# Reordering the load queue of a fused scan and feed-forward kernel: an input block ahead of the first turns

## The chip, the cores and the metric

The kernel runs on one core of a Trainium2 chip. The metric is the device time of one execution in microseconds (us). "Fast" runs are those in which the core was not in its slow state. A core has TensorE (PE, matmuls), VectorE (DVE), ScalarE (ACT), GpSimd (POOL) and SyncE (SP), which here issues nearly all transfers. A transfer that transposes on its way (kind DMA_TRANSPOSE) is called a *turn* below.

## The reference, cut to what matters

```python
xn = layernorm(x)                               # x: 2048 x 512, bf16
Bu = xn @ B_bar.T                               # complex: two real products (B_re, B_im)
h[t] = Lam_bar * h[t-1] + Bu[t]                 # scan over the 2048 rows
y = 2 * Re(h @ C.T) + xn * Dskip
out = x + y + (gelu(xn @ w_gate) * (xn @ w_up)) @ w_down
```

The kernel works in four blocks of 512 rows. Block 0 is special: while the weights still arrive, a *first stage* multiplies centred rows, turned on TensorE itself, with the first 896 columns of the gate and up weights. For the other columns, for Bu and for all later blocks, TensorE reads normalized rows that a turn has brought into the layout it needs.

## The kernel before

The program is written as a list of operations. A planner inside the kernel orders VectorE, ScalarE and GpSimd; **TensorE and SyncE keep the order in which the operations are written**. So the source order of the loads is the order of the load queue.

```python
def tr_par():                                   # the parameter turn: 16 x 128 -> 128 x 16
    S.dma(lambda e: e.dma_start_transpose(PAR..., PROW16.ap), ..., tag="tr_par", issue=900.0)
def TR(b, js=range(4)):                         # the turns of block b, one for each 128 rows
    for j in js:
        S.dma(lambda e, ...: e.dma_start_transpose(XNT[b].ap[:, :, 128*j:128*(j+1)], XN[tt % 8].ap), ...)
...
load_W()                                        # the last weight pieces
tr_par()
...                                             # the first stage
TR(0, [0, 1])
...
TR(0, [2, 3])
ld_x(1)                                         # x of block 1, 512 KB
params()                                        # angles from the parameters
tables_dve(None)
load_B()                                        # B_re, B_im (turns), the D row, x of block 2
LN(1, [0, 1]); LN(1, [2, 3])
TR(1)
SKIP(0)
GU(0, [7, 8, 9, 10])                            # gate/up of block 0, waits for all of TR(0)
...
BU(0)                                           # Bu of block 0
```

Of the kernel before, what the change touches and what calls it, by code (L numbers as in the profile page):

```python
# [352 lines left out]
def d_dve_tt2x(n): return 100.0 + 0.52 * n  # L353
# [4 lines left out]
def d_act(n, ptr=0): return 190.0 + 0.833 * n + 90.0 * ptr  # L358
# [3 lines left out]
def build(nc, ins, out):  # L362
    with ExitStack() as es:
# [113 lines left out]
        def ld_x(b):  # L477
            return S.dma(lambda e, b=b: e.dma_start(
                X_all.ap[:, 4 * b:4 * b + 4, :], x2[512 * b:512 * (b + 1), :].rearrange("(j p) d -> p j d", p=128)),
                512 * 1024, writes=X[4 * b:4 * b + 4], tag="ld_x%d" % b)  # L480
# [28 lines left out]
        def tr_par():  # L509
            S.dma(lambda e: e.dma_start_transpose(PAR.ap.rearrange("p q t -> p (q t)").unsqueeze(1), PROW16.ap), 4096,  # L510
                  reads=PROWq, writes=[PAR], tag="tr_par", issue=900.0)
# [7 lines left out]
        def load_T(bufs, nms):  # L519
            for b_, nm in zip(bufs, nms):  # L520
                S.dma(lambda e, b_=b_, nm=nm: e.dma_start_transpose(b_.ap, ins[nm]),
                      1.4 * 512 * 1024, writes=[b_], tag="tr_" + nm, issue=3000.0)

        def load_W():
            ld_w(WG, WGc, ins["B_w_gate"], 2)
            ld_w(WU, WUc, ins["B_w_up"], 2)

        def load_B():
            load_T([A.sub(BBT_all, "BBTc%d" % c, c) for c in range(2)], ("A_B_re", "A_B_im"))
            S.dma(lambda e: e.dma_start(DSKB.ap, ins["A_Dskip"].unsqueeze(0).broadcast_to([128, D])),  # L530
                  128 * 1024, writes=[DSKB], tag="ld_dsk")
            ld_x(2)

        def load_C():
            load_T(CRAW, ("A_C_re", "A_C_im"))
# [15 lines left out]
        def params():  # L551
            S.order_behind(POOL(lambda e: e.tensor_tensor(DTB.ap, EXB.ap, LDT.ap, ALU.pow), 1100, [EXB, LDT], [DTB], "exp_dt"), GATE["pow"])
            V(lambda e: e.tensor_tensor(pa(TH), DTB.ap, LIM.ap, ALU.mult), D_TINY, [DTB, LIM], [PA[TH]], "th")
            V(lambda e: e.tensor_tensor(pa(A_), DTB.ap, LRE.ap, ALU.mult), D_TINY, [DTB, LRE], [PA[A_]], "a")
            POOL(lambda e: e.tensor_tensor(pa(RRr), EXB.ap, pa(A_), ALU.pow), 1100, [EXB, PA[A_]], [PA[RRr]], "exp_a")
            V(lambda e: e.tensor_scalar(w16(0, 4), pa(TH), 1.0 / TWO_PI, None, ALU.mult), D_TINY, [PA[TH]], [W16p[0]])
            V(lambda e: e.tensor_scalar(w16(4, 8), pa(TH), 512.0 / TWO_PI, None, ALU.mult), D_TINY, [PA[TH]], [W16p[1]])
            V(lambda e: e.tensor_scalar(w16(8, 16), w16(0, 8), 0.25, None, ALU.add), D_TINY, W16p[0:2], W16p[2:4])
            V(lambda e: e.tensor_copy(KI.ap, W16.ap), D_TINY, W16p, [KI])
            V(lambda e: e.tensor_tensor(FRC.ap, W16.ap, KI.ap, ALU.subtract), D_TINY, W16p + [KI], [FRC])  # L560
# [34 lines left out]
        def tables_dve(behind):  # L595
            for s in range(KP):
                V(lambda e, s=s: e.tensor_scalar(K1s[s].ap, IOTJ.ap, W16.ap[:, s:s + 1], None, ALU.mult),
                  d_dve_ts4x(512) * 1.3, [IOTJ, W16p[0]], [K1s[s]], "k1", [GATE["evTA"]])
                V(lambda e, s=s: e.scalar_tensor_tensor(F1s[s].ap, IOTJ.ap, W16.ap[:, s:s + 1], K1s[s].ap, ALU.mult, ALU.subtract),
                  d_dve_1x(512), [IOTJ, W16p[0], K1s[s]], [F1s[s]], "f1")  # L600
            S.order_behind(V(lambda e: e.tensor_scalar(A1.ap.bitcast(I32), F1.ap.bitcast(I32), 0x7FFFFFFF, None, ALU.bitwise_and), d_dve_ts4x(2048) * 2, F1s, [A1], "a1"), behind)
# [6 lines left out]
        def stats(b, j):  # L608
            tt = 4 * b + j
            return (V(lambda e: e.bn_stats(ST[tt].ap, X[tt].ap), d_dve_1x(512), [X[tt]], [ST[tt]], "bnst"),  # L610
                    V(lambda e: e.bn_aggr(MVt[b][j].ap, ST[tt].ap), D_TINY, [ST[tt]], [MVt[b][j]], "bnag"))

        def root(b, j0, j1):
            mn, sbq, qb, rq = (cols(t, b, j0, j1) for t in (MN, SBQ, QB, RQ))
            mv = Buf("MV%d_%d_%d" % (b, j0, j1), "sb", MVt[b][j0].lo, MVt[b][j1 - 1].hi, MV[b].ap[:, j0:j1])
            op = V(lambda e: e.tensor_scalar(sbq.ap, mv.ap[:, :, 1], EPS_BF16, None, ALU.add), D_TINY, [mv], [sbq], "sbq")
            GATE["pow"] = POOL(lambda e: e.tensor_tensor(qb.ap, sbq.ap, HALF.ap[:, 0:j1 - j0], ALU.pow), 1100, [sbq, HALF], [qb], "pow")
            POOL(lambda e: e.tensor_copy(mn.ap, mv.ap[:, :, 0]), 200, [mv], [mn], "mn")
            return op, mn, qb, rq

        def recip(qb, rq):
            return V(lambda e: e.reciprocal(rq.ap, qb.ap), 150, [qb], [rq], "rq")

        def norms(b, js, mn, rq, j0):
            last = None
            for j in js:
                tt, i = 4 * b + j, j - j0
                xs = XN[tt % 8]
                last = S.order_behind(V(lambda e, tt=tt, i=i, xs=xs: e.tensor_scalar(
                    xs.ap, X[tt].ap, mn.ap[:, i:i + 1], rq.ap[:, i:i + 1], ALU.subtract, ALU.mult),  # L630
                  d_dve_ts4x(512), [X[tt], mn, rq], [xs], "ln_n"), last)
            return last

        def LN(b, js=range(4)):
            for j in js:
                stats(b, j)
            _, mn, qb, rq = root(b, js[0], js[-1] + 1)
            recip(qb, rq)
            norms(b, js, mn, rq, js[0])
# [23 lines left out]
        def SKIP(b):  # L663
            for tt in range(4 * b, 4 * b + 4):
                xs = XN[tt % 8]
                V(lambda e, tt=tt, xs=xs: e.tensor_tensor(XD[tt].ap, xs.ap, DSKB.ap, ALU.mult),
                  d_dve_tt2x(512), [xs, DSKB], [XD[tt]], "skip")
# [64 lines left out]
        def TR(b, js=range(4)):  # L732
            for j in js:
                tt = 4 * b + j
                S.dma(lambda e, b=b, j=j, tt=tt: e.dma_start_transpose(
                    XNT[b].ap[:, :, 128 * j:128 * (j + 1)], XN[tt % 8].ap),
                    1.6 * 128 * 1024, reads=[XN[tt % 8]], writes=[XTk[b][j]], tag="tr_x%d" % b, issue=1280.0)
# [212 lines left out]
                     d_dve_ts4x(512), [X[j], MVt[0][j]], [XN[j]], "sub")  # L950
        load_par()
        load_W()
        tr_par()
        S.order_behind(ACT(lambda e: e.activation(H0[3].ap[:, 0:D], X[1].ap, ACTF.Copy, scale=-1.0 / D, accum_out=NM1.ap), d_act(512) + 190,
                           [X[1]], [H0[3], NM1], "mean1"), GATE["par"])

# [54 lines left out]
        norms(0, [2], mn0, rq0, 0)  # L1011
        norms(0, [3], mn3, rq3, 3)
        TR(0, [2, 3])
        ld_x(1)
        params()
        tables_dve(None)
        load_B()
        LN(1, [0, 1]); LN(1, [2, 3])
        TR(1)
        SKIP(0)  # L1020
        GU(0, [7, 8, 9, 10])
        GATE["before_gelu"] = [tables_act([GATE["last_gelu"]])]
# [29 lines left out]
def bass_parallel_sum__ssm_conv_s5__geglu_ffn__prompt_kernel(  # L1052
    nc: bass.Bass,
    A_x: bass.AP,
    A_Lambda_re: bass.AP,
    A_Lambda_im: bass.AP,
    A_B_re: bass.AP,
    A_B_im: bass.AP,
    A_C_re: bass.AP,
    A_C_im: bass.AP,  # L1060
    A_log_dt: bass.AP,
    A_Dskip: bass.AP,
    B_x: bass.AP,
    B_w_gate: bass.AP,
    B_w_up: bass.AP,
    B_w_down: bass.AP,
    out: bass.AP,
):
    ins = {
        "A_x": A_x, "A_Lambda_re": A_Lambda_re, "A_Lambda_im": A_Lambda_im,  # L1070
        "A_B_re": A_B_re, "A_B_im": A_B_im, "A_C_re": A_C_re, "A_C_im": A_C_im,
        "A_log_dt": A_log_dt, "A_Dskip": A_Dskip,
        "B_w_gate": B_w_gate, "B_w_up": B_w_up, "B_w_down": B_w_down,
    }
    build(nc, ins, out)
# [28 lines left out]
```

## Time and profile before

| what | value |
|---|---|
| time | 177.46 us (median of 3), 177.29 (median of 6 with the later runs) |
| TensorE busy | 172.1 us of 175.7 |
| last turn of block 0 lands | 16.99 us |
| gate/up matmuls of block 0 start | 18.24 us by the record |

The prediction below shows the main lines. The chain of waits of the kernel before, in order of time (columns: start, duration, engine and line, count), begins like this.

```profile
0.77 3.15 PE PS L932 x7
3.92 0.11 PE PS L939
4.03 0.13 PE PS L679
4.16 0.30 PE PS L939 x4
...
4.57 0.38 PE PS L700 x2
...
11.26 6.93 PE PS L711 x40
18.18 0.05 issue
18.24 5.13 PE PS L842 x23
```

L932 is the warm-up (matmuls on constants), L939 fills, L679 turns on TensorE, L700 and L711 are the first stage, L842 the gate/up matmuls. Seven warm-up matmuls of 512 columns take 3.15 us, 450 ns each: half the later pace. TensorE's clock is not yet open (more on this below). Two things that I passed over: the pace changes *between* 4.16 and 4.57 us in this run, and L842 has **23** records where the program has 24. The "issue" of 0.05 us ahead of it is the trace of a lost record. The first gate/up matmul was at 18.02 us (one matmul of 0.22 us earlier), not 18.24.

### The profile page before, as it was taken

How to read it: one execution, taken by the hardware profiler on the slowest of the kernel's cores; microseconds unless marked ns; L12 is line 12 of the kernel's file. 1: busy time of each engine (PE TensorE's matmuls, PEld its weight loads, DVE VectorE, ACT ScalarE, POOL GpSimd, SP SyncE). 2: the span in 40 equal slices, each digit the busy share in tenths (PEclk: the TensorE clock that was granted, in tenths of full speed). 3: DMA queues.
4: the chain of work that ended last, by engine and by line, in shares of the span. 5: the costliest groups of instructions: out<-in, count | busy, mean ns of one | idle time of the engine just before them, and what ended most of it. 6: DMA issues, size and time to landing. Idle time of an engine off the chain costs nothing.

```text
span 175.7 us, 2494 instructions
## 1 busy us (share of the span) xinstructions
PE 172.1 (98%) x868; PEld 84.0 (48%) x883; DVE 159.8 (91%) x279; ACT 95.5 (54%) x185; POOL 10.7 (6%) x24
## 2 busy tenths in 40 slices
PE   8999999999999999999999999999999999999995
PEld 3545564644544444444644444444464444444454
DVE  6987999996999989889899999989999899999941
ACT  5476677899876898383576792000667970000000
POOL 3122030201000000002100000000000000000000
DMA  5899999695998000002015000002001000000311
GB/s 155 241 320 174 215 178 222 126 132 113 191 298 225 0 4 2 0 30 85 8 39 111 1 0 0 4 0 90 30 0 30 4 0 0 0 0 0 120 64 60
DMA packets 32420, 14.36 MB, mean 82 GB/s; under 512 B 23736, under 2 KB 32408, under 8 KB 32408
## 3 DMA queue, kind: packets, MB, share of 16 engines
q1 hardware_dynamic: 32240, 14.07, 35.5%
q8 instruction: 7, 0.11, 0.3%
q10 hardware_dynamic: 168, 0.13, 0.2%
q14 instruction: 5, 0.04, 0.1%
HBM read 6.46 MB, written 2.10 MB: 49 GB/s over the span
## 4 chain that ended last, share of the span: by engine, by line
PE 98%; issue 1%; DVE 0%
PE PS L883 37%; PE PS L842 32%; PE PS L748 16%; PE PS L711 4%; PE PS L700 3%; PE PS L816 3%; PE PS L932 2%; PE PS L679 1%; PE PS L939 0%; DVE arena L901 0%
## 5 line engine op out<-in xcount | busy, mean ns | idle before, releaser
L883 PE MATMUL PS<-arena 128*128 128x512 bf16 (+3 forms) x317 | 65.9, 366 | 0.3
L842 PE MATMUL PS<-arena 128*128 128x512 bf16 x257 | 57.1, 379 | 0.4
L883 PEld LDWEIGHTS PS<-arena 128*128 128x128 bf16 (+1 forms) x323 | 30.8, 98 | 35.2
L842 PEld LDWEIGHTS PS<-arena 128*128 128x128 bf16 x264 | 25.8, 98 | 30.2
L786 DVE TENSOR_TENSOR_SCAN arena<-arena 128x512 bf16<-128x512 f32 x32 | 38.9, 1255 | 0.0
L857 ACT ACTIVATE arena<-PS 128x512 bf16<-128x512 f32 x33 | 19.8, 599 | 25.8 <-DVE arena L901 16.7
L748 PE MATMUL PS<-arena 128*128 128x512 bf16 (+1 forms) x134 | 28.0, 366 | 0.1
L861 ACT ACTIVATE arena<-PS 128x512 bf16<-128x512 f32 x33 | 19.8, 600 | 5.1 <-PE PS L842 5.1
L875 ACT ACTIVATE PS<-arena 128x512 f32<-128x512 bf16 (+2 forms) x17 | 9.6, 581 | 19.7 <-DVE arena L901 19.0
L748 PEld LDWEIGHTS PS<-arena 128*128 128x128 bf16 x136 | 13.3, 98 | 14.1
L757 ACT ACTIVATE arena<-PS 128x512 bf16<-128x512 f32 x32 | 17.7, 592 | 2.1 <-PE PS L748 2.1
L901 DVE TENSOR_TENSOR arena<-PS,arena 128x512 bf16<-128x512 f32 (+2 forms) x17 | 10.9, 653 | 6.4 <-PE PS L883 6.4
L863 DVE TENSOR_TENSOR arena<-arena 128x512 bf16<-128x512 bf16 x33 | 13.1, 416 | 1.7 <-ACT arena L861 1.6
L775 DVE TENSOR_TENSOR arena<-arena 128x4096 bf16<-128x4096 bf16 (+1 forms) x5 | 9.2, 1859 | 0.8 <-ACT arena L606 0.8
L773 DVE TENSOR_TENSOR arena<-arena 128x4096 bf16<-128x4096 bf16 (+1 forms) x5 | 9.2, 1859 | 0.1
L798 DVE TENSOR_TENSOR arena<-arena 128x4096 bf16<-128x4096 bf16 x4 | 9.2, 2288 | 0.1
L799 DVE TENSOR_TENSOR arena<-arena 128x4096 bf16<-128x4096 bf16 x4 | 9.1, 2284 | 0.0
L720 ACT ACTIVATE arena<-PS,arena 128x256 bf16<-128x256 f32 (+1 forms) x16 | 6.6, 448 | 3.9 <-PE PS L700 2.1
L610 DVE BATCH_NORM_STATS2 arena<-arena 128x6 f32<-128x512 bf16 x12 | 7.7, 679 | 0.1
L711 PE MATMUL PS<-arena 128*128 128x512 bf16 (+1 forms) x40 | 7.1, 336 | 0.0
L723 DVE SCALAR_TENSOR_TENSOR arena<-PS,arena 128x256 bf16<-128x256 f32 (+1 forms) x16 | 6.3, 445 | 0.5 <-PE PS L700 0.5
L700 PE MATMUL PS<-arena 128*128 128x512 bf16 (+1 forms) x28 | 6.2, 349 | 0.2
(96 smaller groups left out, 124.6 us busy)
## 6 DMA issues: line engine op xcount, KB each, us to landing
out_dram<-arena SPq DMA_DIRECT2D x15, 128.0 KB, 1.7
arena<-in_A_x_dram SPq DMA_DIRECT2D x3, 512.0 KB, 5.3
arena<-in_B_w_down_dram SPq DMA_DIRECT2D x1, 1280.0 KB, 7.2
arena<-in_B_w_gate_dram SPq DMA_DIRECT2D x4, 128.0 KB, 3.0
arena<-in_B_w_up_dram SPq DMA_DIRECT2D x4, 128.0 KB, 3.1
arena<-in_B_w_gate_dram SPq DMA_DIRECT2D x1, 480.0 KB, 6.5
arena<-in_B_w_up_dram SPq DMA_DIRECT2D x1, 480.0 KB, 7.4
arena<-arena SPq DMA_TRANSPOSE x25, 3.1
```

The costliest lines, as they stand in the source:

```text
L700: PE(lambda e: e.matmul(dst, XCd(j, k), WGU[:, ws[0]:ws[-1] + 1, k, f0:f1], start=first, stop=k == KD - 1, skip_group_check=True), d_pe([w ...
L711: ins_ = e.matmul(dst, XCd(j, k), WGU[:, :, k, f0:f1], start=(k == 0), stop=(k == KD - 1))
L748: ins_ = e.matmul(PS[bank][:, 128 * j0:128 * j1], BBT[c][dk].ap[:, 128 * s:128 * (s + 1)], XNT[b].ap[:, dk, 128 * j0:128 * j1], start=(dk ...
L757: GATE["evBu"] = ACT(lambda e, bank=bank, k3=k3, s=s, c=c: e.activation(SSc[k3][s][c].ap, PS[bank][:, :], ACTF.Copy), d_act(512), [BANK[ba ...
L786: V(lambda e, g=g, rb=rb, init=init: e.tensor_tensor_scan(g.ap, rb, g.ap, init, ALU.mult, ALU.add), d_dve_scan(512), [g, PA[RRr]] + ([CARc ...
L842: ins_ = e.matmul(PS[bank][0:m, c0:c1], W.ap[:, dk, 128 * ft:128 * ft + m], XNT[b].ap[:, dk, c0:c1], start=(dk == 0), stop=(dk == KD - 1))
L857: GATE["last_gelu"] = ACT(lambda e, bg=bg, kk=kk, m=m: e.activation(GG[kk].ap[0:m, :], PS[bg][0:m, :], ACTF.Gelu_apprx_tanh), d_act(512), ...
L861: ACT(lambda e, bu=bu, kk=kk, m=m: e.activation(UPB[kk].ap[0:m, :], PS[bu][0:m, :], ACTF.Copy), d_act(512), [BANK[bu]], [UPB[kk]], "evU")
L863: V(lambda e, kk=kk, m=m, ft=ft, k2=k2: e.tensor_tensor(HTt[k2][ft].ap[0:m, :], GG[kk].ap[0:m, :], UPB[kk].ap[0:m, :], ALU.mult), d_dve_tt ...
L875: ACT(lambda e: e.activation(PS[bank][:, c0:c1], X[tt].ap[:, c0:c1], ACTF.Copy), d_act(c1 - c0), [X[tt]], [BANK[bank]], "seed")
L883: ins_ = e.matmul(PS[bank][:, c0:c1], l_[:, 128 * j:128 * (j + 1)], r_[:, c0:c1], start=False, stop=last and n == len(ops) - 1, skip_group ...
L901: V(lambda e: e.tensor_tensor(OUTB[ko].ap[:, c0:c1], PS[bank][:, c0:c1], XD[tt].ap[:, c0:c1], ALU.add), d_dve_1x(c1 - c0), [BANK[bank], XD ...
```

## The change

Its intent: bring x of block 1 in earlier, so that VectorE can begin its normalization, and let what is not urgent (parameters, D row) wait. No instruction is added or removed.

```diff
         def load_B():
             load_T([A.sub(BBT_all, "BBTc%d" % c, c) for c in range(2)], ("A_B_re", "A_B_im"))
+
+        def load_skip():
             S.dma(lambda e: e.dma_start(DSKB.ap, ins["A_Dskip"]...
-            ld_x(2)
@@
         load_W()
-        tr_par()
+        ld_x(1)
@@
         TR(0, [2, 3])
-        ld_x(1)
+        tr_par()
         params()
         tables_dve(None)
         load_B()
+        ld_x(2)
         LN(1, [0, 1]); LN(1, [2, 3])
         TR(1)
+        load_skip()
         SKIP(0)
```

## The prediction

> **What bounds the kernel now.** I read the page's busy times first, then the chain that ended last, then three engine timelines of the first 45 us, because the change touches only the order of loads there.
>
> ```profile
> PE 172.1 (98%) x868; PEld 84.0 (48%) x883; DVE 159.8 (91%) x279; ACT 95.5 (54%) x185; POOL 10.7 (6%) x24
> PE 98%; issue 1%; DVE 0%
> ```
>
> The chain of waits is TensorE (PE) from the first microsecond to the last. A busy row alone could hide pipelined idleness, so I check the pace: the same chain lists 49 matmuls of 512 columns in 10.74 us (219 ns each) in every gate/up stage, and 12 of them in 2.60 us (217 ns) elsewhere. The pace is the same in all stages, and the "issue" pieces between them are 0.05 us, about what a missing record leaves. From 18 us to 174 us TensorE therefore streams without a gap, in an order that the program fixes. The only loose place is before 11 us: the early matmuls between 4.57 and 11.26 us are 12 of 256 columns, 16 of 512 and 16 short transposes. At 219 and some 110 and 55 ns that is 5.7 us of streaming in 6.7 us. So at most about 1 us is there to gain, and it hangs on the first rows of x and the weight pieces, which the change doesn't touch.
>
> The second view is the timeline of the load queue (SyncE; columns: start, time that the queue was taken, line, kind, target and source, count).
>
> ```profile
> 7.51 0.51 SPq L489 DMA_DIRECT2D arena<-in_B_w_up_dram  x1
> 8.14 2.37 SPq L510 DMA_TRANSPOSE arena<-arena  x1
> 10.56 5.18 SPq L735 DMA_TRANSPOSE arena<-arena  x4
> 15.79 0.58 SPq L478 DMA_DIRECT2D arena<-in_A_x_dram  x1
> 16.41 3.06 SPq L521 DMA_TRANSPOSE arena<-in_A_B_re_dram  x1
> 19.51 3.60 SPq L521 DMA_TRANSPOSE arena<-in_A_B_im_dram  x1
> 23.16 0.58 SPq L530 DMA_DIRECT2D arena<-in_A_Dskip_dram  x1
> 23.78 0.43 SPq L478 DMA_DIRECT2D arena<-in_A_x_dram  x1
> 24.34 5.13 SPq L735 DMA_TRANSPOSE arena<-arena  x4
> ```
>
> In this order: last weight piece; the turn (DMA transpose) of the parameters; four turns of block 0; x of block 1; B twice; the D row; x of block 2; four turns of block 1. The third view is TensorE's timeline, which says when each is needed.
>
> ```profile
> 11.10 7.09 PE L711 MATMUL PS<-arena 128*128 128x512 bf16 x40
> 18.24 5.13 PE L842 MATMUL PS<-arena 128*128 128x512 bf16 x23
> 23.20 1.48 PE L816 MATMUL PS<-arena 128*128 128x192 bf16 x16
> 24.52 14.00 PE L748 MATMUL PS<-arena 128*128 128x512 bf16 x70
> ```
>
> The gate/up matmuls of block 0 (L842, at 18.24) need all four turned tiles of block 0. The Bu matmuls (L748, at 24.52) need B_re at once, B_im after the 16 matmuls of the first component (about 28 us), and block 1's turns after all 32 of block 0 (about 31.5 us).
>
> Asking each issue for its time to landing, I get: last weight piece 14.9 us (7.51 + 7.4), parameter turn 15.2, the turns of block 0 at 15.5, 15.9, 16.4, 17.0, x of block 1 at 19.6, B_re 23.8, B_im 25.4, D row 27.7, x of block 2 at 29.1, turns of block 1 at 30.2, 30.7, 31.1, 31.6. So the slack now is 1.2 us at the gate/up matmuls (18.2 - 17.0), some 0.8 us at B_re, and near none at the last turn of block 1. Landings march on in issue order: this queue is a backlog.
>
> **What the Trainium skill says.** "DMA: Bandwidth & Descriptors", section "Queues, rings and completion order": on each DMA engine the descriptors of one queue are consumed in ring order. The trace agrees: issues at 7.51, 8.14 and 10.56 land at 14.9, 15.2 and 15.5. Hence what stands in front delays what stands behind. The same page, section "Issuing engines are not separate DMA queues": all transfers share 16 engines; the trace shows them booked full from 9 to 16 us (DMA share 0.97 to 1.42 in one-microsecond windows), so there is no second road. "Perfetto Trace Analysis", section on the HWDGE DMA instruction: the profiled piece of a DMA is the making of its descriptors, not the move. The trace agrees: 0.5 us for a weight piece that lands 7.4 us later. "TensorE: Matmul & The Clock Gate", section "Back-to-back issue gap", gives about 131 ns a matmul of 512 columns sustained, and 216 ns isolated; this trace shows 217 to 219 sustained, so I take TensorE as having nothing to give.
>
> **The change part by part.** No instruction is added or removed; four loads change places.
>
> (a) x of block 1 (512 KB) goes from behind block 0's turns to before them. It is issued at about 8.1 us and starts to move when the weights are done, at 14.9. Its cost I take from its twin: x of block 2 landed 1.4 us after the D row in front of it; at the 320 GB/s of 10 to 14 us it is 1.6. So it lands at about 16.4 instead of 19.6, 3.2 us earlier.
>
> (b) The turns of block 0 now stand behind those 1.5 us. The twin again: the four turns of block 1 behind x of block 2 landed 1.1 us after it, then every 0.45 us, 2.5 us for the last. Then block 0's last turn lands at 16.4 + 2.5 = 18.9 us, where TensorE wants it at 18.24. That is a stall of **0.6 us**. If only the 1.5 us are added to the old 17.0, it is 18.5 and 0.3 us. As TensorE never waits afterwards, nothing later absorbs it.
>
> (c) The parameter turn goes behind block 0's turns. They wait for normalized rows (the last is written at 13.0), so they issue from about 9.9 to 15 us; the parameter turn issues to 16 or 17.5 and lands at 18.5 to 19.5 in place of 15.2. What hangs on it is a GpSimd power (1.02 us), a few small VectorE (DVE) instructions and the angle tables. Those ended at 30.2 us, because VectorE was full, not because the parameters were late: th was there at 16.52, but the last multiply of the tables came only at 28.8. VectorE now has block 1's statistics (four of 0.65 us) to do meanwhile, so tables and statistics swap. Estimate 0 on the chain.
>
> (d) B is issued at 16 to 17.5 instead of 16.41, but with x of block 1 already landed. Its two issues took 3.06 and 3.60 us behind that load; C, the same shape on an empty queue, landed 4.4 us after issue. So B_re lands at about 21 to 23.5, still before 24.5. Cost 0.
>
> (e) The D row goes last. Its use (L666) is at 33.7 us and has no near consumer on TensorE. Cost 0. Block 1's turns come earlier, but TensorE was not waiting for them. Gain 0.
>
> (f) The program order on VectorE and ScalarE is made by the kernel's own planner, which assumes that loads move at 350 bytes per ns plus 2 us. By its rule x of block 1 would be there about 13.8 us into the span (3.34 MB of earlier loads in 9.55 us, 1.5 us for itself, 2 us, and the start at 0.74), 2.6 us before my 16.4. If it puts a statistics instruction in front of a product of the first stage, VectorE (in order) stands still until the load is there. Those products free PSUM banks: bank 2 was free at 17.0 for a matmul at 18.24, so 1.2 us can be lost unseen, and more while TensorE is stalled for (b). I count 0.1 us on average.
>
> Sum: 177.46 + 0.6 + 0.1 = about **178.1 us**.
>
> **Rivals.** First, nothing happens: the turns still land by 18.2, as 17.0 + 1.2 would. For it: the last turn needed just 2.5 us from issue, and the issues start 0.6 us earlier. Against it: the DMA engines are full. It gives 177.4. Second, VectorE becomes the new wait, by (f): VectorE sits up to 2.6 us and TensorE loses that less 1.2, plus a knock-on at the first output stage, whose C coefficients are ready at 71.65 us and used at 63.85 + 44 x 0.217 = 73.4, only 1.7 us later. That gives 179 to 180.5. For it: the statistics have the room (VectorE had one hole, 15.3 to 16.5); against it: the planner may fill exactly that hole, and then almost nothing is lost. Third, a gain: the intent is surely an earlier block 1 and a fuller VectorE. VectorE at 91% looks near the limit, but the chain shows it with 0%, so an earlier VectorE buys nothing. At best 177.0.
>
> **Range and chances.** The terms span -0.4 (noise; the runs lay at 177.1 to 177.93) to +2.3. I give 177.1 to 179.7. A change of 2% is 3.55 us: a gain of that size doesn't exist on a full TensorE, and a loss would take rivals one and two at their worst together. Faster 0.01, same 0.94, slower 0.05.
>
> **What would show it.** Block 0's gate/up matmuls start at 18.5 to 19 instead of 18.24, with a wait for a DMA before them; after that TensorE runs gapless and every later stage is shifted by the same amount. x of block 1 lands near 16.4, the parameter turn after 18, B_re before 24.5. The prediction is wrong if TensorE waits at the Bu matmuls (B late), if VectorE shows a hole at 14 to 16.5 in front of a statistics instruction (rival two), or if the first output stage waits for the C coefficients.

## The result, and the profile after

The changed kernel took **177.69 us** (median of 6, 177.45 to 177.9) against 177.29 (median of 6, 177.08 to 177.93). The ratio is 1.0018, with a 95% interval of 0.9999 to 1.0037. A ratio is the mean time of one kernel's fast runs over that of the other's of the same rounds, so it is not quite the ratio of the medians. By the ratio the loss is 0.3 us (0.0018 x 177.3), half of the 0.64 us that I had forecast; the interval just includes no loss at all, so this set alone does not show one.

The load queue after (same view as in the prediction):

```profile
7.51 0.65 SPq L489 DMA_DIRECT2D arena<-in_B_w_up_dram  x1
8.20 1.63 SPq L478 DMA_DIRECT2D arena<-in_A_x_dram  x1
10.03 6.16 SPq L736 DMA_TRANSPOSE arena<-arena  x4
16.32 1.15 SPq L510 DMA_TRANSPOSE arena<-arena  x1
17.51 2.82 SPq L521 DMA_TRANSPOSE arena<-in_A_B_re_dram  x1
```

The issue of x of block 1 took 1.63 us where it took 0.58 before; what it waits for, no view says. It landed 7.9 us after its start, at 16.07; the turns landed at 16.57, 17.03, 17.52 and 17.99. So far as foretold, though the turns follow faster. Now the chain of waits after:

```profile
0.77 3.14 PE PS L933 x7
3.92 0.11 PE PS L940
4.02 0.25 PE PS L680
4.28 0.43 PE PS L940 x4
4.70 0.57 PE PS L701 x2
...
11.94 6.93 PE PS L712 x40
18.86 5.18 PE PS L843 x24
24.04 1.32 PE PS L817 x16
25.36 13.83 PE PS L749 x72
```

Line numbers from here on have moved by one. The gate/up matmuls follow the first stage **without a gap**. In this run they did not wait for the turns at all. What is late is the first stage itself: it begins its second part at 11.94 instead of 11.26, and the delay arises before 7 us, in matmuls that ran at half pace (four fills in 0.43 us, not 0.30; a pair of 256 columns in 0.57, not 0.38). Both kernels have issued exactly the same loads up to 8 us. The profiles of before and after thus differ by 0.68 us for a reason that the change cannot have made, while the foretold stall is missing. A verdict from these two profiles would be wrong either way.

The Trainium skill explains the opening: "TensorE: Matmul & The Clock Gate", section "Part 1: The HAM clock gate", says that the array starts at half clock and opens after a busy window of 3.4 us, and that this window is free-running, so that the moment differs from run to run. The traces agree that the moment differs: by the spacing of the matmuls the half pace ended at about 4.2 us in the profile of before and at about 6.7 in that of after, a wider spread than the half microsecond either way that the page gives.

### The profile page after: what moved, and what is told of

It reads as the page before. It is cut to its first block, busy times and chain, and to the rows that moved or that the text cites. A ratio compares the mean times of both kernels' runs of the same rounds, so it can differ in the third digit from the quotient of the medians.

```text
span 176.3 us, 2506 instructions
## 1 busy us (share of the span) xinstructions
PE 173.7 (99%) x883; PEld 84.6 (48%) x883; DVE 160.4 (91%) x279; ACT 95.4 (54%) x185; POOL 9.7 (6%) x24
## 4 chain that ended last, share of the span: by engine, by line
PE 99%; DVE 0%; issue 0%
PE PS L884 37%; PE PS L843 32%; PE PS L749 16%; PE PS L712 4%; PE PS L701 3%; PE PS L817 3%; PE PS L933 2%; PE PS L680 1%; PE PS L940 0%; DVE arena L902 0%
## 5 line engine op out<-in xcount | busy, mean ns | idle before, releaser
L843 PE MATMUL PS<-arena 128*128 128x512 bf16 x264 | 58.1, 379 | 0.0
L749 PE MATMUL PS<-arena 128*128 128x512 bf16 (+1 forms) x136 | 28.1, 366 | 0.0
L712 PE MATMUL PS<-arena 128*128 128x512 bf16 (+1 forms) x40 | 7.1, 336 | 0.0
L701 PE MATMUL PS<-arena 128*128 128x512 bf16 (+1 forms) x28 | 6.9, 380 | 0.0
```

The costliest lines, as they stand in the source:

```text
L701: PE(lambda e: e.matmul(dst, XCd(j, k), WGU[:, ws[0]:ws[-1] + 1, k, f0:f1], start=first, stop=k == KD - 1, skip_group_check=True), d_pe([w ...
L712: ins_ = e.matmul(dst, XCd(j, k), WGU[:, :, k, f0:f1], start=(k == 0), stop=(k == KD - 1))
L749: ins_ = e.matmul(PS[bank][:, 128 * j0:128 * j1], BBT[c][dk].ap[:, 128 * s:128 * (s + 1)], XNT[b].ap[:, dk, 128 * j0:128 * j1], start=(dk ...
L843: ins_ = e.matmul(PS[bank][0:m, c0:c1], W.ap[:, dk, 128 * ft:128 * ft + m], XNT[b].ap[:, dk, c0:c1], start=(dk == 0), stop=(dk == KD - 1))
```

## The experiments

**Theories.** *Clock*: the 0.3 us is chance, the clock's opening alone. *Turns*: the last turn of block 0 lands later, and TensorE waits where the clock opened early. *Parameters*: the late parameter turn costs it, through the tables. Kernels are compared only within the same rounds. Where the expectations count 152.3 us from the Bu matmuls to the end, they take a run's time, which is 1.3 us longer than the span of its profile; the text below counts to the end of the span.

### The two kernels again, and a third time

No edit.

> The kernel before, unchanged, as a null. Clock theory (the 0.3 us between the two kernels is the moment at which TensorE's clock opens in the first 7 us, which differs from run to run and which the order of loads does not touch): ratio 1.000 within 0.002, single runs spread over 177.0 to 177.95, and in the profile the last first-stage matmul is followed by the first gate/up matmul without a gap, both shifted by whatever the first 7 us took. Turn theory (block 0's turns land later in the changed kernel and hold TensorE): the same for this run.

> The changed kernel, unchanged. Clock theory: its runs spread over the same 177.0 to 177.95 as the kernel before, with some below 177.3, and the mean ratio is 0.999 to 1.001 once there are more runs. Turn theory: no run below 177.4, mean ratio 1.002, and a profile in which the clock opened early shows TensorE waiting up to 0.3 us before the first gate/up matmul.

> The changed kernel a third time, for the distribution. Two-path theory with packet hits: most runs 177.3 to 177.9, none below 177.2, and about one run in six near 179. If the profiled run is one of those near 179, its 16 KB instruction packet lies before the landing of the last turn, and that turn lands near 20; if it is an ordinary run, the packet lies after it.

The kernel before against itself: ratio 1.0001 (0.9987 to 1.0016), runs 177.16 to 177.63. The changed kernel: 177.66, 178.84, 179.04, 177.58, 177.34, 177.74, ratio 1.0044 (1.0012 to 1.0077), and the third time 177.6 to 178.22, ratio 1.0023 (1.0009 to 1.0036). Of 17 runs of the changed kernel none is below 177.34; the kernel before had one at 177.2 or below. **The clock theory as the whole cause falls.** My forecast of a run near 179 in the third set missed too: it had none, its highest was 178.22.

The profile of the second set caught an early opening. TensorE's timeline:

```profile
11.32 7.09 PE L712 MATMUL PS<-arena 128*128 128x512 bf16 x40
18.70 5.34 PE L843 MATMUL PS<-arena 128*128 128x512 bf16 x24 [0.29 <-DMA arena<-arena]
```

and the answer for the last turn of block 0 (issued at 15.50 us):

```profile
L736 SPq DMA_TRANSPOSE arena<-arena x1: 1265/1265/1265, 15.5 to 15.5; - x1
...
  PE PS L843: 0.3, 1
...
DMA to landing us min/median/max: 3.1/3.1/3.1
```

In the brackets stands what ended TensorE's idle time: a transfer from SBUF to SBUF, the turn. It landed at 18.57, and the first gate/up matmul is 0.13 us behind it. In the profile after, the first stage's second part ran from 11.77 to the first gate/up matmul at 18.70, which is 6.93 us; 11.32 + 6.93 = 18.25. So 0.45 us was lost here. This is the stall of the prediction. (The last turn was also issued later, at 15.50 us instead of 14.48, and took 3.07 us to land instead of 2.52: x in front held up both.)

### One part at a time

x of block 1 early, all else as before:

```diff
         load_W()
         tr_par()
+        ld_x(1)
@@
         TR(0, [2, 3])
-        ld_x(1)
```

> One part alone: x of block 1 goes before block 0's turns, the parameter turn stays ahead of both, the D row and x of block 2 stay. Turn theory (end time = 152.3 us after the start of the Bu matmuls, and that start is the later of two paths: first-stage matmuls done, 18.2 to 18.9 us by the clock's opening, or the last turn landed plus 0.13): the last turn lands 1 to 1.5 us later than before, at 18.0 to 18.6, so no run below 177.3, median 177.6, ratio 1.001 to 1.003. If x in front costs nothing: ratio 1.000, runs from 177.05.

177.74 us (177.45 to 177.9), ratio 1.0038 (1.0025 to 1.0051). The last turn landed at 18.33, and TensorE's timeline shows the same wait:

```profile
11.04 7.09 PE L711 MATMUL PS<-arena 128*128 128x512 bf16 x40
18.46 5.34 PE L842 MATMUL PS<-arena 128*128 128x512 bf16 x24 [0.33 <-DMA arena<-arena]
```

Within the noise, this part alone makes the whole loss.

The reverse, the changed kernel with only this part undone:

```diff
         load_W()
-        ld_x(1)
@@
         TR(0, [2, 3])
+        ld_x(1)
         tr_par()
```

> The changed kernel with one part undone: x of block 1 goes back behind block 0's turns (turns, x of block 1, parameter turn, B, x of block 2, turns of block 1, D row). Two-path theory: the last turn lands at 16.7 to 17.2, no wait, times 177.0 to 177.7, ratio 1.000 within 0.0015; if the instruction packet falls on the turns, as in the kernel with only the parameter turn late, it lands near 18.4 and the times are 177.5 to 177.7. Rival (the late parameters cost the time): 177.6 and no late turn.

177.28 us (177.04 to 177.69), ratio 1.0009 (0.9994 to 1.0023). The last turn landed at 17.27 and nothing waited:

```profile
11.34 7.09 PE L712 MATMUL PS<-arena 128*128 128x512 bf16 x40
18.27 5.34 PE L843 MATMUL PS<-arena 128*128 128x512 bf16 x24
```

The runs reach down to 177.04 again, with the parameters and the D row as late as in the changed kernel. It doesn't beat the kernel before; it equals it.

The D row alone (moved behind block 1's turns; x of block 2 directly behind B, as in the change; cut):

```diff
         def load_B():
             load_T([A.sub(BBT_all, "BBTc%d" % c, c) for c in range(2)], ("A_B_re", "A_B_im"))
+            ld_x(2)
+
+        def load_skip():
             S.dma(lambda e: e.dma_start(DSKB.ap, ins["A_Dskip"]...
-            ld_x(2)
@@
         TR(1)
+        load_skip()
```

> One part alone: only the D row moves behind block 1's turns, x of block 2 before it. All of it happens after the gate/up matmuls of block 0 have started. Expected 0 by every theory: ratio 1.000 within 0.0015, start of Bu matmuls to the end 152.3 us.

177.37 us, ratio 0.9995 (0.9982 to 1.0008): nothing, as expected.

The parameter turn alone:

```diff
         load_W()
-        tr_par()
@@
         TR(0, [2, 3])
+        tr_par()
         ld_x(1)
```

> One part alone: only the parameter turn moves behind block 0's turns; x of block 1 stays behind them. Clock theory: ratio 1.000 within 0.002, spread as before. Parameter rival (late parameters push the angle tables and with them the first scan chain and the C coefficients, which had 1.7 us of slack before the first output stage): ratio 1.002 or more, and a wait of TensorE in the first output stage.

This was the surprise: 177.67 us in a band of 177.57 to 177.72, ratio 1.0019 (1.0004 to 1.0033), with x of block 1 *behind* the turns. The ratio lies just inside what the clock theory allowed (1.000 within 0.002), but the spread does not: it had promised runs from 177.0 on. The parameter theory nearly had the number (1.002 or more), but not the wait: TensorE shows none in the first output stage. The turns landed at 15.45, 15.92, 16.41 and then **18.44**, and TensorE again started 0.13 us later:

```profile
18.57 5.34 PE L842 MATMUL PS<-arena 128*128 128x512 bf16 x24 [0.30 <-DMA arena<-arena]
```

The trace's records of single DMA packets show one thing on the fourth turn's way: from 16.16 to 17.26 us a packet of 16 KB on another queue. It is of the kind that the page lists as instructions (of the kernel before):

```profile
q8 instruction: 7, 0.11, 0.3%
```

Seven packets, 0.11 MB: 16 KB each. From 16.25 us on, the 256-byte packets of the turns, up to then some 160 to 280 in each quarter of a microsecond, trickled at 4 to 9 for 0.75 us. The same thin stretch follows the first such packet in other profiles, where no TensorE wait hangs on it: in the kernel before, half a microsecond after its first packet at 20.11 us, five quarters in a row have 1 to 10.

### The instruction packets

The Trainium skill, "Runtime: NRT & Kernel Launch", section "Instruction fetch mechanics", says that each engine's instructions come in blocks of 16 KiB, 256 instructions, through a DMA queue of its own, and calls the cost mostly hidden. If the packets are TensorE's, more matmuls at the start must move them. A first hint is on the page of the profile: TensorE has 868 matmuls and 883 weight loads, 1751 instructions or 6.8 blocks of 256, and no other engine has more than 279. In three kernels I replaced the warm-up matmuls by four times as many, a quarter as wide: the same time on TensorE, 21 matmuls (42 instructions with their weight loads) more.

```diff
-            for _ in range(nwarm):
-                ins_ = e.matmul(PS[wb][:, :], ones, ones4, start=True, stop=True)
+            for _ in range(4 * nwarm):
+                ins_ = e.matmul(PS[wb][:, 0:128], ones, ones, start=True, stop=True)
```

> Control: the kernel before with the 28 short warm-up matmuls. Its last turn has 1.2 us of slack, so an earlier instruction packet should cost nothing: ratio 1.000 within 0.002, runs 177.0 to 177.7. If short matmuls warm the clock worse, its runs all lie in the upper part, 177.5 to 177.9.

> The kernel with only the parameter turn late, where a 16 KB instruction packet (1.1 us long) at 16.16 us coincided with the last turn landing at 18.44 instead of about 16.9. Here the 7 warm-up matmuls of 512 columns are 28 of 128: the same TensorE time, 21 more matmuls in the instruction stream. Fetch theory (these packets are TensorE's own instructions, one per 256 of them; the first falls by chance on the turns): all instruction packets come earlier (by about 42 instructions, some 4 us in steady stages), the last turn lands before 17.3, single runs spread over 177.05 to 177.7 again, median 177.3. Rival (the parameter turn behind it delays the last turn by itself): packets move, but the last turn still lands at 18.4 and the times stay within 177.55 to 177.75.

> The changed kernel with the same 28 short warm-up matmuls. Fetch theory: no runs near 179 (two of six had 178.84 and 179.04, which I put down to the packet falling on the last turn), the last turn lands at 18.0 to 18.6, times 177.3 to 177.8. Rival: the 179 runs come from something else and appear here too, in a third of the runs.

| kernel | its runs, us | ratio | first packet, us | last turn lands |
|---|---|---|---|---|
| before, 28 short | 177.14 to 178.14 | 1.0023 (1.0008 to 1.0039) | 20.30 | 17.03 |
| parameter turn late, 28 short | 177.29 to 178.36 | 1.0026 (1.0009 to 1.0044) | 17.45 | 16.88 |
| changed, 28 short | 177.48, 177.69, 178.84, 179.03, 179.25, 179.4 | 1.0083 (1.0051 to 1.0115) | 15.36 | 20.32 |

Packets two to seven came earlier, in the kernel before (against its second profile, "before again") by 3.0 us (35.71 to 32.67) for the second and by 4.3 to 4.9 for the others. 256 instructions take some 26 us in steady stages, so 42 should move them by 4.3. Between these packets of "before again", TensorE's records count 243 to 268 instructions. They are TensorE's instructions. The first packet did not obey: it stayed at 20.3 in one kernel, came later in another (17.45, not 16.16) and earlier in the third (15.36, where the three profiles of the changed kernel have 18.88 to 21.17). What sets its moment stays open.

In the second row the packet fell behind the last turn, and the turn was on time, as the fetch theory wanted; that the mean still lay 0.26% up was not expected, and the control row shows the same, so the short warm-up has a small cost of its own. In the third row my expectation was wrong in its direction: the packet came *earlier* and fell in front of the turns. It was 2.45 us long; the first turn then landed 1.87 us after x of block 1, where the three profiles of the changed kernel have 0.50 to 0.53, and all four were late. TensorE's timeline of this run of 179.4 us:

```profile
11.28 7.09 PE L712 MATMUL PS<-arena 128*128 128x512 bf16 x40
20.46 5.34 PE L843 MATMUL PS<-arena 128*128 128x512 bf16 x24 [2.09 <-DVE arena L612]
```

The bracket names a small VectorE instruction that ended just before; the last turn landed at 20.32, and 20.46 is the usual 0.13 to 0.14 us later. I take the turn for the cause, because the rule of the last table below fits it to the hundredth. So in these profiles an instruction block that comes through while the turns do goes with some 1.4 to 1.5 us of later landing (1.87 less 0.5 here, 2.03 less 0.5 above). Of the 2.25 us that TensorE lost in this run, I put these 1.4 down to the block; the other 0.85 are left for x in front. That the two runs at 178.84 and 179.04 of the changed kernel had this too is likely, not shown: they were not profiled.

### A double dose

x of block 2 goes ahead of block 0's turns as well.

```diff
         load_W()
-        ld_x(1)
+        ld_x(1); ld_x(2)
@@
         load_B()
-        ld_x(2)
```

> Double dose: x of block 2 is loaded before block 0's turns as well. In the changed kernel the last of these turns landed at 17.99 us and the gate/up matmuls could start at 18.24 (clock opened early) or 18.86 (late). Another 512 KB in front at about 330 GB/s adds 1.6 us, so the last turn lands at 19.6. Both theories then expect TensorE to wait for the turns: start of the gate/up matmuls at about 19.7 in either clock state, time 178.5 to 178.7, and almost no spread between runs, because the wait swallows the clock. If it stays at 177.7 the turns are not what gates these matmuls.

181.12 us (180.38 to 182.4), ratio 1.0225 (1.0189 to 1.026): more than either theory's 178.6, and not tight. The first three turns landed at 18.43, 18.92 and 19.43, as expected; the fourth at 21.44, with an instruction packet at 19.28. TensorE stood still, and then something new came. TensorE in stretches (busy time, granted clock, DMA share, GB/s):

```profile
18.00:20.00 2.00, 0.83 (x6) 1.00 0.88 171
20.00:21.50 1.50, 0.00 (x0) 1.00 0.03 6
21.50:22.00 0.50, 0.42 (x2) 1.00 0.76 179
22.00:22.50 0.50, 0.50 (x3) 0.67 1.19 222
22.50:25.00 2.50, 2.50 (x7) 0.50 1.28 228
25.00:27.00 2.00, 2.00 (x10) 0.85 0.98 206
```

TensorE was idle for 2.75 us, began again at 21.58, and only then, near 22.2 us, did the clock fall to half. It stayed there until about 25.6 (0.67 and 0.85 are means over stretches in which it changed), and the gate/up matmuls took 7.03 us, not 5.18 (chain). A stall of TensorE is thus not linear: here it cost its own time and about 1.7 us more.

That is not certain to happen. In two of the six runs the mean clock on record is 1.0; their spans are 179.1 and 179.3 us, and the rule of the last table gives 28.07 + 151.14 = 179.2, if their turns landed as in this profile. The other four runs have 0.99. What decides can be worked out from the clock records of the traces. Here they change at 5.10, 22.17 and 25.58 us, which is five times and once 3.41 us apart. In the 3.41 us before 22.17 TensorE worked for only 0.7 us (until 18.83 and from 21.58). The changed kernel with 28 short matmuls also stood idle, from about 18.2 to 20.46, and kept its clock: its record of 5.41 us, in steps of 3.41, puts a boundary at 19.06, in the middle of the idle stretch. So it seems to count whether the idleness falls into one such stretch; two profiles are no proof.

### Clearing the gate

If the gate at the first gate/up matmul is all, then making TensorE come later must hide the order. In both kernels:

```diff
-        nwarm = 7
+        nwarm = 9       # in a second pair: 12
```

> The kernel before with 9 instead of 7 warm-up matmuls: TensorE's first real work starts 0.85 us later, part of which is swallowed by its waits for weights. Two-path theory: the gate/up matmuls start at 18.5 to 19.3 us instead of 18.2 to 18.9, times 177.4 to 178.1, no DMA wait in front of them. This is the base for the next run.

> The changed kernel with 9 warm-up matmuls. Two-path theory: TensorE now comes to the gate/up matmuls after the last turn has landed (18.0 to 18.6), so the order of loads costs nothing: median equal to that of the kernel before with 9 warm-up matmuls within 0.2 us, except for single runs near 179 in which the instruction packet holds a turn back. Rival (the order costs something elsewhere, in VectorE or behind the Bu matmuls): still 0.3 to 0.5 us slower than the kernel before with 9.

> The kernel before with 12 warm-up matmuls, base for the next run. Start of the Bu matmuls = start of the first stage's later half (11.1 to 11.8 us with 7) + 13.42 + what 5 more warm-up matmuls add after the waits for weights (1.1 to 2.1 us, less some 0.6): 25.2 to 26.6 us; the end 151.14 us after it; times 177.8 to 179.2.

> The changed kernel with 12 warm-up matmuls. Two-path theory: the last turn lands at 18.0 to 18.9, TensorE asks for it at 18.9 to 20, so no wait in front of the first gate/up matmul, and the median equals that of the kernel before with 12 within 0.15 us (single runs 1.2 us longer if the packet hits the turns). Rival (a cost elsewhere than at this gate): 0.3 to 0.5 us slower, as with 7 and with 9.

With 9: before 177.65 (177.2 to 177.92), changed 178.04 (177.55 to 178.09). The changed one is still slower, against the expectation and by as much as the rival (a fixed cost elsewhere) had said, though its profile shows no wait: the last turn landed at 18.81, TensorE came at 19.06 (19.28 less one lost record). The profiled pair differs by 0.37 us before that, in the start of the first stage's second part (12.13 against 11.76). With 12: before 178.71 (178.42 to 178.87), changed 177.92 (177.59 to 179.07). The sign has turned. In the profiled runs the 12 warm-up matmuls took 4.96 us before and 4.13 us after, so the clock opened earlier in the second; that is larger than the effect I was after. The rival would have left the changed kernel 0.3 to 0.5 us slower, and my own theory had said "within 0.15 us"; both missed, because the clock swamped the pair. These four runs settle little alone; it is the next table that speaks against a cost elsewhere.

### What all seventeen profiles say together

Two numbers can be read from every profile: when the first stage's second part started (S; L711, or L712 in the changed kernels) and when the last turn of block 0 landed (T). From the profile of before, the Bu matmuls start at S + 13.42 (24.52 - 11.10). From that of the changed kernel's second set, at T + 6.63 (25.20 - 18.57). Then the end should follow the later of the two.

| profiled run | S | T | S+13.42 | T+6.63 | Bu start | run, us |
|---|---|---|---|---|---|---|
| before | 11.10 | 16.99 | **24.52** | 23.62 | 24.52 | 176.98 |
| before again | 11.60 | 17.20 | **25.02** | 23.83 | 25.02 | 177.48 |
| D row late | 11.74 | 16.75 | **25.16** | 23.38 | 25.16 | 177.62 |
| before, 28 short | 11.37 | 17.03 | **24.79** | 23.66 | 24.80 | 177.25 |
| before, 9 warm | 11.76 | 17.35 | **25.18** | 23.98 | 25.19 | 177.65 |
| before, 12 warm | 12.54 | 17.72 | **25.96** | 24.35 | 25.97 | 178.42 |
| x of block 1 early | 11.04 | 18.33 | 24.46 | **24.96** | 24.96 | 177.45 |
| parameter turn late | 11.19 | 18.44 | 24.61 | **25.07** | 25.07 | 177.67 |
| the same, 28 short | 11.20 | 16.88 | **24.62** | 23.51 | 24.62 | 177.29 |
| changed | 11.77 | 17.99 | **25.19** | 24.62 | 25.20 | 177.67 |
| changed, again | 11.32 | 18.57 | 24.74 | **25.20** | 25.20 | 177.66 |
| changed, third | 11.50 | 18.75 | 24.92 | **25.38** | 25.39 | 177.84 |
| changed, 28 short | 11.28 | 20.32 | 24.70 | **26.95** | 26.95 | 179.40 |
| changed, 9 warm | 12.13 | 18.81 | **25.55** | 25.44 | 25.56 | 178.04 |
| changed, 12 warm | 11.72 | 18.46 | **25.14** | 25.09 | 25.14 | 177.60 |
| changed, x behind the turns | 11.34 | 17.27 | **24.76** | 23.90 | 24.77 | 177.25 |
| changed, x of 1 and 2 first | 11.74 | 21.44 | 25.16 | **28.07** | 29.76 | 182.21 |

The larger of the two (bold) is the start of the Bu matmuls within 0.01 us in all but the last row, where the clock fell. And from that start to the end of the span it is 151.13 to 151.17 us in fifteen of the seventeen; the two with only the parameter turn late have 151.28 and 151.32, and for the first of these the 0.14 us lies behind the last matmul, at the last store. For the second, with the 28 short matmuls, the 0.18 us lies before the last matmul, and no single wait of TensorE shows it. But for these two, everything that the order of loads does to the time in these profiles, it does before the Bu matmuls, at one gate.

## Why the prediction was right or wrong, point by point

The measured 177.69 us lies in the range, and the place and the mechanism were right. The size was not: the loss by the ratio was 0.3 us, and 0.64 had been forecast.

- **TensorE is the bound and nothing later absorbs or adds:** right; 151.13 to 151.17 us from the Bu matmuls to the end.
- **(a) x of block 1 at 16.4 us:** right; 16.07, 16.59 and 16.77 in the three profiles of the changed kernel.
- **(b) is the step that failed**, in both of its terms. "2.5 us for the last" turn behind x came from the twin in block 1; measured were 1.92, 1.98 and 1.98 us, because the first turn followed x by 0.5 us, not 1.1 (the later ones every 0.46 to 0.50, about as predicted); why the twin was slower, no run shows. So the last turn landed at 17.99 to 18.75, not at 18.9. And "TensorE wants it at 18.24" took one profile's number, spoilt by a lost record, for a constant. TensorE comes at S + 6.93, which is 18.25 to 18.70 in these three runs and 18.02 in the profile of before: the clock moves it by more than half a microsecond. The stall was 0, 0.46 and 0.47 us in place of 0.6, on the mean 0.31. Mechanism and place were right; a difference of two moments was taken where the mean of a maximum was needed. The other sum in (b), which was set aside (18.5 us, a stall of 0.3), came nearer: the three landings have a mean of 18.44. In the third profile the view names another releaser:

```profile
19.10 5.13 PE L843 MATMUL PS<-arena 128*128 128x512 bf16 x23 [0.52 <-ACT arena L721]
```

  One of the 24 records is lost, so the first matmul was at 18.88 (its weight load is at 18.86), 0.13 us behind the turn at 18.75; the ScalarE instruction named ended only at 19.07.
- **(c) parameters:** they landed at 20.94, 19.12 and 19.30 (18.5 to 19.5 foretold), at no cost in the changed kernel. That moving them alone can put an instruction block onto the turns was not foreseen.
- **(d) B:** cost 0, but B_re landed at 23.36, 24.78 and 24.97, in two of three profiles later than the 21 to 23.5 foretold. In the third profile 0.42 us of slack was left.
- **(e) D row and block 1's turns:** right, 0.9995 for the D row alone.
- **(f) and the second rival:** the planner did as feared. VectorE in the changed kernel's third profile:

```profile
14.97 0.74 DVE L724 SCALAR_TENSOR_TENSOR arena<-PS,arena 128x256 bf16<-128x256 f32 x2
16.79 0.69 DVE L611 BATCH_NORM_STATS2 arena<-arena 128x6 f32<-128x512 bf16 x1 [1.08 <-DMA arena<-in_A_x_dram]
17.40 1.37 DVE L724 SCALAR_TENSOR_TENSOR arena<-PS,arena 128x256 bf16<-128x256 f32 x4
```

  VectorE stood for 1.08 us before block 1's statistics, with first-stage products behind them. The second profile has the same 1.08 us, the first none. The prediction had named such a hole as a sign of being wrong, so this sign appeared. But TensorE did not wait for VectorE: the gate/up matmuls started by the turn's rule, 18.75 + 0.13. The 0.1 us that I counted was not seen. Nor was it in the changed kernels with 9 and 12 warm-up matmuls: there VectorE stood for 0.54 and 0.61 us, the turns were in time, and the Bu matmuls still started within 0.01 us of S + 13.42.
- **The first rival (nothing happens)** holds in the runs where the clock opens late, as in the first profile. That is why the loss is smaller than the forecast stall.
- **Small readings:** the opening has 8 matmuls of 256 columns and 20 of 512, not 12 and 16 (one merged group was misread), so about 0.6 us was loose there, not 1; the slack at B_re was 0.72 us; the GB/s from 10 to 14 us have a mean of 335. None of this moves the sum.

## What to carry to other kernels

Before a load is moved ahead, look for what stands behind it in the same queue and ask how much slack its consumer has: here 512 KB in front of four small turns ate 1.2 us of slack at the gate of an engine that never idles, for an earlier input that nobody waited for. Compare that slack with the spread of the consumer's own arrival over several runs, not with one profile: the cost is the mean of the later of two moments. And when two profiles differ by as little as their own kernel's runs do, let one part at a time, timed often, decide, and the trace only say where.

## What the Trainium skill lacked or had wrong

- "TensorE: Matmul & The Clock Gate", section "Back-to-back issue gap", gives some 131 ns as the sustained spacing of 512-column matmuls. The runs show 216 ns (76 in 16.42 us in the profile after), which is the page's isolated figure.
- "Runtime: NRT & Kernel Launch", section "Instruction fetch mechanics", calls the cost of a 16 KiB block mostly hidden; what it does to other transfers is not said. Here TensorE's blocks took 0.88 to 3.0 us on the DMA engines. Where one met the turns, a turn landed 1.4 to 1.5 us later, and the kernel lost 0.46 us (parameter turn late) and some 1.4 us (changed, 28 short).
- No page says that a profile's granted clock can read 1.00 in the opening, although in the profile after four fills took 0.43 us in place of 0.22 (four short transposes at full pace). Its first clock record is at 6.70 us, so the 1.00 before it rests on no record. After an idle stretch the view does show the fall (0.50).
- The clock page gives an idle window of about 3.4 us for the fall. In the double dose an idle stretch of 2.75 us was enough; the fall came some 0.6 us after TensorE had begun again, lasted about 3.4 us and cost about 1.7 us (29.76 against 28.07).
- No page says why the issue of the same plain load takes so different a time: x of block 1 took 0.58 us behind block 0's turns, 0.57 behind the parameter turn (x early alone) and 1.01 to 1.85 behind the weights. The runs do not show the cause.
